# A three-stage kernel whose order comes from a planner: costs set to traced durations, first steps reordered, one integer step moved to ScalarE

## The chip, the cores and the metric

One core of one Trainium2 chip. The metric is the device time of one execution in microseconds (us). Of three runs of the kernel before, the median is 1590.36 us (1588.12 to 1594.29).

## The reference, cut to what matters

```python
def _attn_ref(q, k, v, p):            # batch 8, heads 8, seq 576, head_dim 64; p has 32 rows
    p_packed = sm_attn(p, k, v)       # 32 packed queries attend to k, v
    return sm_attn(q, p_packed, p_packed)
...
x = attn_out.transpose(0, 2, 1, 3).reshape(B * S, H * D)     # 4608 x 512
g = x @ w_gate; x = (g * sigmoid(g) * (x @ w_val)) @ w_out   # d_ff 1536
h = x @ w_in; g = where(h >= 1, h, where(h <= -1, 0, (h + 1) ** 2 / 4))
out = g @ w2_out                                             # d_ff 2048
```

All of it is float32, but the weights of the two MLPs arrive as 64-bit floats.

## The kernel before, in words

**Tiles and stages.** The attention runs in 16 "quads" (a batch and four heads). A quad has four steps: `stage_a` (scores of the packed rows and exponentials), `stage_b` (transposes and values), `stage_c` (scores of q) and `stage_d` (outputs). The two MLPs are products of 9 blocks of 512 tokens with pairs of weight columns. A "unit" (`first_unit`) is seven Strassen products of 12 matmuls, each 128x128 by 128x256 (line 1171); second products are at lines 1315 (512 columns) and 1433. Each operand is a high and a low half in float16, so every product is three matmuls. To make an operand, its block of four quarters in a `raw` buffer is scaled (`copy`, lines 392 and 396), summed into the quarters that Strassen's scheme needs (`either`, line 378), cast to the high halves (`copy`, 390 and 394) and subtracted to give the low halves (378).

**Weights.** A 64-bit weight is two 32-bit words. `from_words` makes a float32 of them: ScalarE rescales the high word (442), VectorE shifts the result left by three (445), and VectorE ors in the upper three bits of the low word (448). It runs on 128x512 at a time, 42 times for the first MLP and 32 for the second. The items of the first MLP are "in" (two columns, four such blocks), "out" and "again" (two blocks each).

**What sets the order.** The program is first recorded as operations with costs per engine, due times and dependencies; `Order.run` then plays it through with a list scheduler, picks an engine for each operation that may run on several, and emits the instructions in that order. On the chip each engine runs its list strictly in order and waits by semaphores, so a wrong cost shows up as a wait. In `copy`, `either` and `act` the costs are written as a constant and a term per column. `QUEUED` bounds how far the transfers on SP run ahead; `PORT` and `AHEAD` say when VectorE prefers an operation that does not share its port with GpSimd. `BEGIN` lists the first steps by letter and number (l load keys and values, q load queries, a to d the attention steps, w convert weights, p prepare them). `LATE` gives the place at which each further weight item of the first MLP is prepared (a place is half a unit; its items are in 1, out 1, in 2, out 2, again 0 to 2, in 3 to 5, out 3 to 5), `NEXT` and `SPACE` the places of the further quads, `CHUNKS` and `CHUNK_SPACE` those of the second MLP's weights.

Of the kernel before, what the change touches and what calls it, by code (L numbers as in the profile page):

```python
# [13 lines left out]
I32 = mybir.dt.int32  # L14
AF = mybir.ActivationFunctionType
# [27 lines left out]
class Order:  # L43
# [225 lines left out]
def packed_attention_then_two_mlps(ctx, tc, qT, kT, v, pT, w1, wo, w2, wo2, out):  # L269
# [111 lines left out]
    def copy(n, dst, src, r, w, late=None, scale=None, psum=False):  # L381
        costs = {
            "ACT": (0.05 if psum else 0.1) + (0.09 if scale else 0.0) + n * 0.00083,
            "DVE": 0.07 + (0.06 if scale else 0.0) + n * (0.00104 if psum else 0.00052),
        }

        def emit(e):
            if e == "ACT":
                if scale is None:
                    nc.scalar.copy(dst(), src())  # L390
                else:
                    nc.scalar.activation(dst(), src(), AF.Copy, scale=scale())  # L392
# [19 lines left out]
    SUM_WAIT, PREP_SUM, PREP_LO, ATT_WAIT, X_LO = 0.0, 4.8, 1.0, 4.0, 0.6  # L412
    HIDDEN_LO, BEND_WAIT = 2.0, 0.5
# [5 lines left out]
    def dma(size, dst, src, r, w, late=None):  # L419
        o.add({"SP": size / 0.3}, lambda e: nc.sync.dma_start(out=dst(), in_=src()), r, w, late)  # L420
# [8 lines left out]
    def flat(b, n=7 * N // 2, dtype=F32):  # L429
        return b.t.rearrange("p a n -> p (a n)").bitcast(dtype)[:, :n]  # L430


    def from_words(words, dst, r, w, n):

        def bits():
            return dst().bitcast(I32)  # L440

        act(n, lambda: nc.scalar.activation(
            dst(), words()[:, :, 1].bitcast(F32), AF.Prelu, scale=2.0 ** -112, alpha=-2.0 ** 32
        ), r, w, fixed=0.12)
        dve(n // 2, lambda: nc.vector.tensor_scalar(
            out=bits(), in0=bits(), scalar1=3, scalar2=None, op0=ALU.logical_shift_left,
        ), w, w, fixed=0.0, shared=True)
        dve(n, lambda: nc.vector.scalar_tensor_tensor(  # L448
            bits(), words()[:, :, 0], 29, bits(), op0=ALU.logical_shift_right, op1=ALU.bitwise_or,
        ), r + w, w, fixed=0.06, shared=True)  # L450
# [299 lines left out]
    def stage_a(i):  # L750
# [3 lines left out]
        for u in range(2):  # L754
            dve(H2, lambda u=u: nc.vector.tensor_reduce(
                t.t[:, u:u + 1], s1[u].t[:, :H2], axis=AX.X, op=ALU.max
            ), [(s1[u], 0)], [(t, u)], 1.0, 0.0)
# [118 lines left out]
    def stage_c(i):  # L876
# [11 lines left out]
        for u in range(2):  # L888
            dve(H2, lambda u=u: nc.vector.transpose(
                flat(zt, S)[:, u * H2:(u + 1) * H2], s2[u].t[:, :H2]  # L890
            ), [(s2[u], 0)], [(zt, u)], 1.0, 0.0)
        dve(S, lambda: nc.vector.tensor_reduce(t.t[:, :NTB], blocks(), axis=AX.X, op=ALU.max),
            [(zt, 0), (zt, 1)], [(t, 0)], None, 0.0)
# [3 lines left out]
            [(zt, 0)], [(zt, 0)], None, "exp", 0.1)  # L897
# [4 lines left out]
            [(zt, 0)], [(t, 1)], None, 0.0)  # L902
# [6 lines left out]
        dve(S, lambda: nc.vector.transpose(flat(z, S), flat(zt, S)), [(zt, 0)], [(z, 0)], None, 0.0)  # L909
# [59 lines left out]
    BEGIN = "l0 a0 w0 l1 p0 q0 q1 a1 b0 w1 c0 p1 b1 d0 c1 d1"  # L969

    FIRST, EARLY = 2, 2
    LATE = (0, 0.5, 4.5, 7, 18, 21, 24, 12, 26, 36, 43, 48, 52)
    LEAD, FETCH = 2, 4
    NEXT, SPACE, AHEAD = (0, 0.9, 2.1, 4.3, 6.2, 8.5, 11), 2.8, 1.2
    CHUNKS, CHUNK_SPACE, BEHIND = 61, 1.25, 0
# [784 lines left out]
```

## Time and profile before

| what | value |
|---|---|
| median of three runs | 1590.36 us |
| the profiled execution | 1590.13 us, of which the span is 1588.2 us |
| TensorE (PE) busy, share of the span | 1530.0 us, 96% |
| VectorE (DVE) busy | 1256.0 us, 79% |
| ScalarE (ACT) busy | 1000.9 us, 63% |
| GpSimd (POOL) busy | 1210.1 us, 76% |
| mean granted TensorE clock | 0.985 |

The profiled execution lies 0.23 us under the median, so a sum against it may be read as one against the median. Its 1.9 us outside the span are not seen in the profile. PE is the engine that ends the kernel; a share of 96% over the whole span hides that nearly all of its idle time lies in the first 200 us, so the table of stretches is to be read before any mean.

### The profile page before, as it was taken

How to read it: one execution, taken by the hardware profiler on the slowest of the kernel's cores; microseconds unless marked ns; L12 is line 12 of the kernel's file. 1: busy time of each engine (PE TensorE's matmuls, PEld its weight loads, DVE VectorE, ACT ScalarE, POOL GpSimd, SP SyncE). 2: the span in 40 equal slices, each digit the busy share in tenths (PEclk: the TensorE clock that was granted, in tenths of full speed). 3: DMA queues.
4: the chain of work that ended last, by engine and by line, in shares of the span. 5: the costliest groups of instructions: out<-in, count | busy, mean ns of one | idle time of the engine just before them, and what ended most of it. 6: DMA issues, size and time to landing. Idle time of an engine off the chain costs nothing.

```text
span 1588.2 us, 36548 instructions
## 1 busy us (share of the span) xinstructions
PE 1530.0 (96%) x14412; PEld 1295.4 (82%) x14412; DVE 1256.0 (79%) x2014; ACT 1000.9 (63%) x1747; POOL 1210.1 (76%) x1042
## 2 busy tenths in 40 slices
PE   5779999999999999999999999999999999999999
PEld 2446676677888889888888888888888888888888
DVE  7988888777877557788778998988777988875674
ACT  5777687767667545776676766656445555654541
POOL 4755577567986546976878998989788888986884
PEclk7889999999999999999999999999999999999999
DMA  9657886665547655977776943343533652254412
GB/s 342 201 189 262 275 289 237 235 225 189 199 136 257 239 166 191 300 263 256 265 250 219 325 149 127 106 173 121 170 100 124 226 180 97 107 188 155 139 59 80
DMA packets 145228, 310.15 MB, mean 195 GB/s; under 512 B 14752, under 2 KB 56224, under 8 KB 145056
## 3 DMA queue, kind: packets, MB, share of 16 engines
q1 hardware_dynamic: 145056, 307.81, 56.8%
q8 instruction: 113, 1.85, 0.5%
q14 instruction: 59, 0.48, 0.1%
HBM read 190.32 MB, written 117.44 MB: 194 GB/s over the span
## 4 chain that ended last, share of the span: by engine, by line
PE 84%; DVE 7%; ACT 5%; DMA 2%; issue 1%; POOL 1%; SPq 0%; ACTq 0%; DVEq 0%
PE ps L1171 46%; PE ps L1433 30%; PE ps L1315 4%; ACT op L390 1%; PE ps L741 1%; DVE op L378 1%; DMA h<-in_w 1%; DVE raw L378 1%; PE ps L940 1%; POOL op L378 1%; ACT raw L392 1%; DVE raw L448 1%; PE ps L786 0%; DVE ps L1154 0%; DVE acc L1333 0%
## 5 line engine op out<-in xcount | busy, mean ns | idle before, releaser
L1171 PE MATMUL ps<-op,op 128*128 128x256 f16 x7560 | 914.8, 273 | 6.6 <-DVE h L1154 4.1
L1171 PEld LDWEIGHTS <-op 128*128 128x128 f16 x7560 | 738.1, 98 | 108.8 <-issue 16.1
L1433 PE MATMUL ps<-op,op 128*128 128x256 f16 x4662 | 583.5, 273 | 1.0 <-POOL op L378 1.0
L378 POOL TENSOR_TENSOR op<-h,op 128x512 f16<-128x512 f32 (+2 forms) x353 | 437.7, 1257 | 125.3 <-ACT op L390 101.1
L1433 PEld LDWEIGHTS <-op 128*128 128x128 f16 x4662 | 456.0, 98 | 54.1 <-POOL op L378 1.5
L390 ACT CAST op<-h 128x512 f16<-128x512 f32 (+2 forms) x372 | 208.0, 596 | 90.4 <-POOL h L378 33.0
L378 POOL TENSOR_TENSOR raw<-raw 128x256 f32<-128x256 f32 (+1 forms) x184 | 177.3, 976 | 44.1 <-ACT raw L392 30.1
L378 POOL TENSOR_TENSOR h<-h,h 128x512 f32<-128x512 f32 (+1 forms) x178 | 203.9, 1146 | 8.2 <-DVE op L378 3.1
L1333 DVE SCALAR_TENSOR_TENSOR acc<-ps,f,acc 128x512 f32<-128x512 f32 x181 | 134.6, 744 | 71.1 <-PE ps L1433 65.9
L392 ACT ACTIVATE p<-ps,f 128x512 f32<-128x512 f32 x172 | 117.4, 686 | 104.5 <-PE ps L1171 97.3
L1546 ACT ACTIVATE ps<-m,half,f 128x512 f32<-128x512 f32 x144 | 112.3, 780 | 102.9 <-POOL m L1543 59.3
L378 POOL TENSOR_TENSOR op<-raw,op 128x512 f16<-128x512 f32 (+3 forms) x102 | 151.2, 1500 | 12.4 <-ACT op L390 10.0
L1549 DVE SCALAR_TENSOR_TENSOR h<-ps,f,h 128x512 f32<-128x512 f32 x144 | 106.3, 742 | 30.3 <-ACT ps L1546 29.8
L378 POOL TENSOR_TENSOR h<-h 128x512 f32<-128x512 f32 x69 | 90.3, 1308 | 47.5 <-DVE h L1518 30.7
L1154 DVE SCALAR_TENSOR_TENSOR h<-ps,f,p 128x512 f32<-128x512 f32 x126 | 93.5, 744 | 39.0 <-PE ps L1171 36.0
L1543 POOL TENSOR_SCALAR m<-h,f 128x512 f32<-128x512 f32 x76 | 63.2, 832 | 51.1 <-ACT ps L1546 31.6
L378 DVE TENSOR_TENSOR op<-h,op 128x512 f16<-128x512 f32 (+1 forms) x82 | 96.0, 1181 | 0.0
L390 ACT CAST op<-raw 128x512 f16<-128x512 f32 (+3 forms) x140 | 88.7, 668 | 9.6 <-POOL raw L378 5.4
L378 DVE TENSOR_TENSOR op<-raw,op 128x512 f16<-128x512 f32 (+3 forms) x66 | 89.8, 1372 | 1.4 <-ACT op L390 1.3
L1315 PE MATMUL ps<-op,op 128*128 128x512 f16 x360 | 86.9, 379 | 0.0
L392 ACT ACTIVATE u<-ps,f 128x512 f32<-128x512 f32 x90 | 61.7, 685 | 38.6 <-PE ps L1171 38.0
L378 POOL TENSOR_TENSOR op<-op,t 128x576 f32<-128x576 f32 x32 | 41.7, 1304 | 53.1 <-DVE t L906 13.4
(151 smaller groups left out, 1631.8 us busy)
## 6 DMA issues: line engine op xcount, KB each, us to landing
xsp<-op SPq DMA_DIRECT2D x72, 448.0 KB, 3.8
op<-xsp SPq DMA_DIRECT2D x72, 448.0 KB, 6.3
sums<-acc SPq DMA_DIRECT2D x88, 256.0 KB, 2.8
acc<-sums SPq DMA_DIRECT2D x88, 256.0 KB, 3.7
op<-wsp_out SPq DMA_DIRECT2D x44, 448.0 KB, 5.2
op<-wsp SPq DMA_DIRECT2D x44, 448.0 KB, 5.1
h<-in_w SPq DMA_DIRECT2D x24, 512.0 KB, 5.8
op<-in_kT SPq DMA_DIRECT2D x32, 288.0 KB, 5.3
```

The source lines that it names most:

```text
L378: lambda e: engine(e).tensor_tensor(dst(), x(), y(), op=op), r, w, late,
L390: nc.scalar.copy(dst(), src())
L392: nc.scalar.activation(dst(), src(), AF.Copy, scale=scale())
L448: dve(n, lambda: nc.vector.scalar_tensor_tensor(bits(), words()[:, :, 0], 29, bits(), op0=ALU.logical_shift_right, op1=ALU.bitwise_or,), r ...
L1154: psum_dve(T, lambda: nc.vector.scalar_tensor_tensor(dst(), lanes(bank.t), self.r(), lanes(add.t), op0=ALU.mult, op1=ALU.add), [(bank, 0), ...
L1171: nc.tensor.matmul(dst, a, b, start=start, stop=stop, skip_group_check=True)
L1315: nc.tensor.matmul(bank.t, x[:, js], y, start=first and i == 0 and m == 0, stop=last and i == 1 and m == 2,)
L1333: psum_dve(T, lambda: nc.vector.scalar_tensor_tensor(acc.t, bank.t, pw.output()(), acc.t, op0=ALU.mult, op1=ALU.add), r + [(acc, 0)], [(ac ...
L1433: nc.tensor.matmul(bank.t[:, l * N:(l + 1) * N], x, y, start=first and l == 0 and m == 0, stop=last and l == 1 and m == 2, skip_group_chec ...
L1543: o.add({"POOL": 0.85, "DVE": 0.42}, lambda e: engine(e).tensor_scalar(out=lanes(m.t), in0=dst(), scalar1=top(), scalar2=low(), op0=ALU.mi ...
L1546: act(T, lambda: nc.scalar.activation(bank.t, m.t, AF.Square, bias=half_one[:, 0:1], scale=inv()), [(m, 0), (f, 0)], [(bank, 0)], fixed=0.35)
L1549: psum_dve(T, lambda: nc.vector.scalar_tensor_tensor(dst(), lanes(bank.t), top(), dst(), op0=ALU.mult, op1=ALU.max), [(bank, 0), (h, t), ( ...
```

## The change

Four things change together. (1) The planner's costs: a copy on ACT costs 0.1 us more, the activations and several VectorE operations get another constant, a transfer runs at 0.39 instead of 0.30 (MB per us), and three of the scheduler's bounds move. (2) The order of the first steps. (3) The places of weight items, quads and chunks. (4) In `from_words` the shift of line 445 goes; a second activation turns the upper 16 bits of the low word into its top three bits, in place, and one VectorE instruction shifts and ors.

```diff
-    QUEUED = 6.4
+    QUEUED = 4.04
...
-    PORT, AHEAD = 0.1, 8.0
+    PORT, AHEAD = 0.33, 10.16
...
     def copy(n, dst, src, r, w, late=None, scale=None, psum=False):
         costs = {
-            "ACT": (0.05 if psum else 0.1) + (0.09 if scale else 0.0) + n * 0.00083,
+            "ACT": (0.16 if psum else 0.2) + (0.11 if scale else 0.0) + n * 0.00083,
...
-        o.add({"SP": size / 0.3}, lambda e: nc.sync.dma_start(out=dst(), in_=src()), r, w, late)
+        o.add({"SP": size / 0.39}, lambda e: nc.sync.dma_start(out=dst(), in_=src()), r, w, late)
...
         act(n, lambda: nc.scalar.activation(
             dst(), words()[:, :, 1].bitcast(F32), AF.Prelu, scale=2.0 ** -112, alpha=-2.0 ** 32
-        ), r, w, fixed=0.12)
-        dve(n // 2, lambda: nc.vector.tensor_scalar(
-            out=bits(), in0=bits(), scalar1=3, scalar2=None, op0=ALU.logical_shift_left,
-        ), w, w, fixed=0.0, shared=True)
+        ), r, w, fixed=0.24)
+        act(n, lambda: nc.scalar.activation(
+            words()[:, :, 0], words().bitcast(U16)[:, :, 1], AF.Copy, scale=2.0 ** -13, bias=2.0 ** -15 - 0.5
+        ), r, r, fixed=0.24)
         dve(n, lambda: nc.vector.scalar_tensor_tensor(
-            bits(), words()[:, :, 0], 29, bits(), op0=ALU.logical_shift_right, op1=ALU.bitwise_or,
+            bits(), bits(), 3, words()[:, :, 0], op0=ALU.logical_shift_left, op1=ALU.bitwise_or,
         ), r + w, w, fixed=0.06, shared=True)
...
-    BEGIN = "l0 a0 w0 l1 p0 q0 q1 a1 b0 w1 c0 p1 b1 d0 c1 d1"
+    BEGIN = "l0 l1 a0 w0 p0 q0 q1 a1 b0 w1 p1 b1 c0 d0 c1 d1"
...
-    LATE = (0, 0.5, 4.5, 7, 18, 21, 24, 12, 26, 36, 43, 48, 52)
-    LEAD, FETCH = 2, 4
-    NEXT, SPACE, AHEAD = (0, 0.9, 2.1, 4.3, 6.2, 8.5, 11), 2.8, 1.2
-    CHUNKS, CHUNK_SPACE, BEHIND = 61, 1.25, 0
+    LATE = (0, 2.5, 4.5, 7, 12, 16, 21, 24, 27, 37, 42.5, 47, 52)
+    LEAD, FETCH = 2, 5
+    NEXT, SPACE, AHEAD = (0, 0.9, 2.1, 4.3, 6, 8.3, 11), 2.8, 0.8
+    CHUNKS, CHUNK_SPACE, BEHIND = 61, 1.22, 0
```

Left out are constants of a few reductions, transposes and one exponential in `stage_a` and `stage_c` (0.07 to 0.1 us more each). Two inserted lines shift the numbers: line 448 of before is 450 now, 1171 is 1173.

Nearly every row of every list moves. Three places show what the prediction speaks of. First ACT, the start of its list (`h` holds the 64-bit words of the first weight item, `raw` the float32, `ps` PSUM tiles, `op` operands). Before:

```order
L442 ACT_TABLE_LOAD
L442 ACTIVATE raw_138<-h_142 128x512
L442 ACTIVATE raw_138<-h_143 128x512
L763 ACTIVATE op_107,t_178<-ps_155,t_178 128x288
L442 ACTIVATE raw_139<-h_144 128x512
L763 ACTIVATE op_107,t_178<-ps_156,t_178 128x288
L442 ACTIVATE raw_139<-h_145 128x512
L390 COPY op_109<-ps_157 128x512
```

Now:

```order
L444 ACT_TABLE_LOAD
L444 ACTIVATE raw_138<-h_142 128x512
L447 ACTIVATE h_142<-h_142 128x512
L444 ACTIVATE raw_138<-h_143 128x512
L447 ACTIVATE h_143<-h_143 128x512
L444 ACTIVATE raw_139<-h_144 128x512
L765 ACTIVATE op_107,t_178<-ps_155,t_178 128x288
L444 ACTIVATE raw_139<-h_145 128x512
L765 ACTIVATE op_107,t_178<-ps_156,t_178 128x288
L447 ACTIVATE h_144<-h_144 128x512
L447 ACTIVATE h_145<-h_145 128x512
```

Four activations have come in, and the first quad's exponentials (line 765, before 763) stand behind five activations of the weights instead of two. Second DVE, the same place, after its memsets. Before:

```order
L755 TENSOR_REDUCE t_178<-ps_155 128x1
L445 TENSOR_SCALAR raw_138<-raw_138 128x512
L755 TENSOR_REDUCE t_178<-ps_156 128x1
L448 SCALAR_TENSOR_TENSOR raw_138<-h_142,raw_138 128x512
L758 TENSOR_SCALAR t_178<-t_178 128x1
L445 TENSOR_SCALAR raw_138<-raw_138 128x512
L448 SCALAR_TENSOR_TENSOR raw_138<-h_143,raw_138 128x512
L445 TENSOR_SCALAR raw_139<-raw_139 128x512 x2
```

Now:

```order
L757 TENSOR_REDUCE t_178<-ps_155 128x1
L757 TENSOR_REDUCE t_178<-ps_156 128x1
L450 SCALAR_TENSOR_TENSOR raw_138<-raw_138,h_142 128x512
L760 TENSOR_SCALAR t_178<-t_178 128x1
L450 SCALAR_TENSOR_TENSOR raw_138<-raw_138,h_143 128x512
L769 TENSOR_SCALAR t_178<-t_178 128x1
L757 TENSOR_REDUCE t_179<-ps_157 128x1
L450 SCALAR_TENSOR_TENSOR raw_139<-raw_139,h_144 128x512
```

The shifts are gone, and the reductions of the second quad (`t_179`) stand earlier. Third PE, after the second products of the second unit (1315, now 1317), where the third unit starts (1171, now 1173) and a quad's `stage_b` stands (786, 805, 829; now 788, 807). Before:

```order
L1315 MATMUL ps_155<-op_126,op_104 128x512
L786 MATMUL ps_159<-ident,op_101 128x128 x4
L786 MATMUL ps_160<-ident,op_101 64x128
L805 MATMUL ps_156<-op_125,op_117 32x64 x4
L805 MATMUL ps_156<-op_137,op_117 32x64 x4
L805 MATMUL ps_156<-op_100,op_117 32x64 x12
L829 MATMUL ps_158<-ident,pp_175 128x128
L835 MATMUL ps_157<-ident,ppsq 1x128
...
L1171 MATMUL ps_161<-op_134,op_119 128x256
```

Now:

```order
L1317 MATMUL ps_156<-op_125,op_109 128x512
L788 MATMUL ps_157<-ident,op_136 128x128 x4
...
L1173 MATMUL ps_159<-op_104,op_121 128x256
...
L1173 MATMUL ps_161<-op_106,op_122 128x256
L788 MATMUL ps_155<-ident,op_136 64x128
...
L1173 MATMUL ps_161<-op_106,op_122 128x256
L807 MATMUL ps_162<-op_120,op_107 32x64 x4
```

48 products of the third unit now stand ahead of the quad's value products (807), which stood ahead of all of them.

## Rows read from the trace of the kernel before

**Rows 1.** The page: an engine's busy time; PE's and clock's rows of the 40 slices.

```profile
PE 1530.0 (96%) x14412; PEld 1295.4 (82%) x14412; DVE 1256.0 (79%) x2014; ACT 1000.9 (63%) x1747; POOL 1210.1 (76%) x1042
...
PE   5779999999999999999999999999999999999999
...
PEclk7889999999999999999999999999999999999999
```

**Rows 2.** Busy time by stretch: length, busy us (instructions) of each engine, clock, DMA.

```profile
0.00:53.70 53.70, 29.20 (x325) 15.16 (x325) 42.25 (x154) 34.77 (x80) 27.12 (x29) 0.78 0.87 295
53.70:114.40 60.70, 44.70 (x475) 29.39 (x472) 54.99 (x122) 50.19 (x99) 42.89 (x35) 0.87 0.62 210
114.40:200.00 85.60, 79.03 (x800) 54.91 (x797) 70.50 (x168) 59.95 (x115) 47.12 (x41) 0.97 0.78 262
200.00:400.00 200.00, 196.49 (x1989) 139.90 (x1988) 159.90 (x304) 153.42 (x285) 142.76 (x120) 1.00 0.69 235
400.00:1500.00 1100.00, 1096.25 (x10063) 980.74 (x10062) 877.69 (x1206) 670.09 (x1118) 893.58 (x770) 1.00 0.54 186
```

**Rows 3.** The chain that ended last, from 1570 us: start, length, what.

```profile
1569.91 14.42 PE ps L1433 x132
...
1584.36 0.75 DVE acc L1333
```

**Rows 4.** DVE in order of time, its first row after the memsets.

```profile
8.44 0.43 DVE L445 TENSOR_SCALAR raw<-raw 128x512 int32<-128x512 int32 x1 [1.83 <-ACT raw L442]
```

**Rows 5.** PE in order of time, 97 to 119 us: start, length, idle before and releaser.

```profile
106.63 1.08 PE L805 MATMUL ps<-op,op 128*32 128x64 f32 x32 [3.30 <-ACT op L390]
108.77 0.44 PE L805 MATMUL ps<-op,op 64*32 64x64 f32 x8 [1.06 <-ACT op L390]
113.93 0.48 PE L829 MATMUL ps<-ident,pp 128*128 128x128 f32 x1 [4.72 <-ACT pp L392]
...
114.41 1.06 PE L1171 MATMUL ps<-op,op 128*128 128x256 f16 x4
115.96 3.27 PE L1171 MATMUL ps<-op,op 128*128 128x256 f16 x16 [0.49 <-DVE op L378]
```

**Rows 6.** Busy time by stretch around the low clock, columns as in rows 2.

```profile
71.00:78.00 7.00, 6.15 (x41) 2.53 (x42) 5.27 (x22) 4.40 (x13) 6.34 (x7) 0.51 0.38 119
...
102.30:114.40 12.10, 2.97 (x47) 1.85 (x48) 11.49 (x14) 10.03 (x18) 11.14 (x9) 0.62 0.58 210
114.40:119.00 4.60, 4.11 (x22) 2.75 (x20) 3.25 (x5) 1.40 (x4) 2.12 (x3) 0.52 0.25 100
```

**Rows 7.** DVE's groups by form, 0 to 114.4 us: count | busy us, mean ns | idle; last line whole span.

```profile
L445 DVE TENSOR_SCALAR raw<-raw 128x512 int32<-128x512 int32 x16 | 9.4, 595 | 2.9 <-ACT raw L442 2.9
L378 DVE TENSOR_TENSOR op<-raw,op 128x512 f16<-128x512 f32 x7 | 7.8, 1111 | 0.0
L378 DVE TENSOR_TENSOR op<-raw,op 128x768 f16<-128x768 f32 x3 | 5.0, 1671 | 0.0
L378 DVE TENSOR_TENSOR op<-raw,op 128x1024 f16<-128x1024 f32 x1 | 2.4, 2367 | 0.0
...
L394 DVE CAST op<-raw 128x512 f16<-128x512 f32 x12 | 11.2, 931 | 0.0
```

**Rows 8.** ACT's groups by form, 0 to 114.4 us, columns as above; last line whole span.

```profile
L442 ACT ACTIVATE raw<-h 128x512 f32<-128x512 f32 x16 | 10.3, 668 | 6.4 <-DMA h<-in_w 6.4
L390 ACT CAST op<-raw 128x512 f16<-128x512 f32 x16 | 9.6, 624 | 2.4 <-DVE raw L378 1.4 <-POOL raw L378 1.0
L392 ACT ACTIVATE raw<-raw,a1s 128x1024 f32<-128x1024 f32 x5 | 5.7, 1146 | 0.9 <-DVE a1s L460 0.9
L390 ACT CAST op<-raw 128x768 f16<-128x768 f32 x5 | 4.1, 822 | 0.0
L390 ACT COPY op<-ps 128x512 f32<-128x512 f32 x6 | 3.5, 585 | 0.9 <-PE ps L786 0.8
...
L1546 ACT ACTIVATE ps<-m,half,f 128x512 f32<-128x512 f32 x144 | 112.3, 780 | 102.9 <-POOL m L1543 59.3
```

More of the change, by code (lines that the diff above doesn't have):

```diff
@@ L14 @@
 I32 = mybir.dt.int32
+U16 = mybir.dt.uint16
 AF = mybir.ActivationFunctionType
@@ L411, in packed_attention_then_two_mlps @@
     COPY_WAITS = {'DVE': 1.0}
-    SUM_WAIT, PREP_SUM, PREP_LO, ATT_WAIT, X_LO = 0.0, 4.8, 1.0, 4.0, 0.6
-    HIDDEN_LO, BEND_WAIT = 2.0, 0.5
+    SUM_WAIT, PREP_SUM, PREP_LO, ATT_WAIT, X_LO = 0, 4.8, 1, 4, 0.6
+    HIDDEN_LO, BEND_WAIT = 2, 0.5
     SQUARE_WAITS = {'DVE': 4.0, 'POOL': 1.0}
@@ L756, in stage_a @@
                 t.t[:, u:u + 1], s1[u].t[:, :H2], axis=AX.X, op=ALU.max
-            ), [(s1[u], 0)], [(t, u)], 1.0, 0.0)
+            ), [(s1[u], 0)], [(t, u)], 1.0, 0.07)
         dve(1, lambda: nc.vector.tensor_scalar(
@@ L890, in stage_c @@
                 flat(zt, S)[:, u * H2:(u + 1) * H2], s2[u].t[:, :H2]
-            ), [(s2[u], 0)], [(zt, u)], 1.0, 0.0)
+            ), [(s2[u], 0)], [(zt, u)], 1.0, 0.1)
         dve(S, lambda: nc.vector.tensor_reduce(t.t[:, :NTB], blocks(), axis=AX.X, op=ALU.max),
-            [(zt, 0), (zt, 1)], [(t, 0)], None, 0.0)
+            [(zt, 0), (zt, 1)], [(t, 0)], None, 0.07)
         either(S, blocks, blocks, lambda: wide(0), sub, [(zt, 0), (zt, 1), (t, 0)], [(zt, 0)], None,
@@ L896, in stage_c @@
         act(S, lambda: nc.scalar.activation(blocks(), blocks(), AF.Exp, scale=SCALE),
-            [(zt, 0)], [(zt, 0)], None, "exp", 0.1)
+            [(zt, 0)], [(zt, 0)], None, "exp", 0.2)
         s = lambda: t.t[:, NTB:2 * NTB]
         dve(S, lambda: nc.vector.tensor_reduce(s(), blocks(), axis=AX.X, op=ALU.add),
-            [(zt, 0)], [(t, 1)], None, 0.0)
+            [(zt, 0)], [(t, 1)], None, 0.07)
         dve(NTB, lambda: nc.vector.tensor_scalar(
@@ L908, in stage_c @@
                ATT_WAIT)
-        dve(S, lambda: nc.vector.transpose(flat(z, S), flat(zt, S)), [(zt, 0)], [(z, 0)], None, 0.0)
+        dve(S, lambda: nc.vector.transpose(flat(z, S), flat(zt, S)), [(zt, 0)], [(z, 0)], None, 0.1)
         z2 = zt
```

## The prediction

> **What bounds the kernel now.** The page comes first. PE is busy for 96% of the span, and the row of slices shows where the other 4% lie: slices one to three are at five and seven tenths, all later ones at nine [rows 1]. The table of stretches puts numbers on it [rows 2]. Up to 53.7 us, where the first MLP product starts, PE idles 53.7 - 29.2 = 24.5 us; from there to 114.4 us it idles 16.0 us; to 200 us 6.6 us; from 200 to 400 us 3.5 us; from 400 to 1500 us 3.8 us in 1100. So 40.5 us of some 58 us of idle time lie before 114.4 us, and whatever the change does after 200 us to engines other than PE can give back 7.3 us at most. The end is one run of products and a last sum on DVE [rows 3], which the change doesn't touch.
>
> Why PE waits early is read from the same table: up to 114.4 us DVE works 42.3 + 55.0 = 97.2 us, which is 85% of the stretch and 92% of what is left after its first work on weights at 8.4 us [rows 4]. ACT works 34.8 + 50.2 = 85.0 us, POOL 70.0 us [rows 2]. PE in order of time shows the form that the wait takes at its worst place: before the third unit PE waits 3.30, 1.06 and 4.72 us, 9.1 us together, in a quad's `stage_b` for results of ACT, and then 0.49 us for DVE [rows 5]. ACT is the name on the wait, but DVE is the engine without a pause in that stretch, 11.5 of 12.1 us, and ACT's casts waited longest for DVE's sums [rows 6, 8].
>
> **The change part by part.** I count up to the first product of the third unit, at 114.4 us, because there the early stage ends: after it PE is nearly full.
>
> *The shift on DVE.* Up to that product 16 blocks of weights are converted in both orders. Their 16 shifts took 9.4 us of DVE [rows 7]. All go: -9.4 us of DVE's work.
>
> *The new activation.* No row shows it. It has 512 columns, so the nearest rows bound it: 0.585 us for a copy out of PSUM below, 0.780 us for the square at line 1546 above [rows 8]. I take 0.668 us, the other activation that reads the same words at the same stride. ACT gains 16 x 0.668 = 10.7 us, at the bounds 9.4 or 12.5 us.
>
> At the start of ACT's list the first quad's exponentials now stand behind three more activations, so 2.0 us later at most, and PE's first transposes wait for them; I count 0, because the first MLP product, at 53.7 us, waits on DVE's later work, and take the 2.0 us into the range.
>
> *What else changes engine.* The planner now prices a 512-column cast on ACT at 0.2 + 512 x 0.00083 = 0.625 us, which the row gives as 0.624 us [rows 8]; before it believed 0.525. It therefore moves work off ACT, and the order shows what: up to the same product ACT loses four casts of 768 columns at 0.822 us, three scalings of 1024 at 1.146 us and two casts of 512 at 0.624 us, together 8.0 us. DVE gains one subtraction of 1024 columns at 2.37 us, four casts of 512 at 0.93 us and a few of under 0.8 us, and loses three subtractions of 768 columns at 1.67 us and two of 512 at 1.11 us to POOL [rows 7]: 6.1 against 7.2 us. The small ones are a dozen and partly cancel; I put them at +1.8 us by an estimate of 0.15 us each, so that +0.7 us is left, give or take 2 us. So DVE's sum falls by 8.7 us to 88.5 us, and ACT's rises by 2.7 us at most, to 87.7 us.
>
> How much of the 8.7 us reaches PE has two ends: nothing, if ACT now holds the same places, and all of it. DVE is the engine nearest to full, so I take all: **-8.7 us** by 114 us.
>
> *The order on PE.* 48 products of the third unit now stand ahead of the value products for which PE waited 9.1 us. I count nothing for that: the fifth of those products itself waited for a subtraction on DVE that ended at 115.9 us [rows 5], so in front they would have waited for it too. What it could give beyond DVE's share is the attention work that now follows, 1.08 + 0.44 + 0.48 = 2.0 us at most.
>
> *The first loads.* On SP the first 15 transfers are the same; then the two blocks of the first output weights pass one load of values, and one block of the next weights falls behind three. In the first stretch DMA is at 0.87 of its time [rows 2], so a later load shifts what waits for it, but the total is the same. I count 0, with 1 us either way.
>
> *The clock.* The granted clock was 0.51 from 71 to 78 us, 0.62 from 102.3 to 114.4 us and 0.52 from 114.4 to 119 us, so PE ran at 1.2 instead of 2.4 GHz in parts of them; the last two lie in and behind the long waits of PE [rows 5, 6]. PE's busy 6.15, 2.97 and 4.11 us there would take 3.1, 1.1 and 2.0 us less at full clock: 6.2 us. The waits removed, 8.7 of 40.5 us, are about a fifth; I take a quarter of the clock's loss back: **-1.5 us**, with 0 and -6.2 us as ends. The Trainium skill says (TensorE: Matmul & The Clock Gate, What's actually happening) that the array gets either all or half of its clock pulses by how busy it has been, so an idle stretch costs a second time in the work after it. By that rule taken at full, as if no wait were left long enough, the sum would be 4.7 us lower, 1575.3 us; the trace agrees that low clock stands behind waits, not how much of them is enough.
>
> *From 114 to 200 us.* Places move: again 0 to 2 come forward (18 to 12, 21 to 16, 24 to 21), in 3 goes back from 12 to 24. An "again" is two blocks, an "in" four, and each brings sums and casts. PE idles 6.6 us here and DVE works 70.5 of 85.6 us [rows 2]; I count 0, and 4 us either way.
>
> *After 200 us.* Here ACT gets 58 more activations and DVE loses 58 shifts. ACT worked 670 of 1100 us, PE 1096 [rows 2]: the cover is PE's own work, and if it were gone, ACT's 58 x 0.67 = 39 us would show only where ACT is on a unit's path. 0, with a gain of 4 us (half of what PE idles) or a loss of 4 us as ends.
>
> Sum, against the profiled 1590.1 us: -8.7 - 1.5 = -10.2, so **1580 us**. The median of the runs, 1590.36 us, is the same within 0.3 us.
>
> **The rivals.**
>
> *ACT takes DVE's place.* Both activations now stand before each or, on a strictly ordered engine, and PE's named waits were for ACT already [rows 5]. If half of the 10.7 us falls on the path, -8.7 becomes -3.4 and the clock gives nothing: 1586.7 us; if all does, 1592 us. For it: ACT's sum of 87.7 us is level with DVE's. Against: it was at 85.0 us before and not the full engine. The Trainium skill (ScalarE: Activation LUTs, Rules for kernel authors) advises VectorE, not ScalarE, for plain arithmetic. By the rows the step itself is dearer, 0.668 against 0.595 us [rows 7, 8], so by that rule alone the time would be 16 x 0.073 = 1.2 us longer, 1591.3 us; the trace doesn't bear it out as long as DVE is the fuller engine.
>
> *The early gain is larger.* DVE pauses for some 9 us between 8.4 and 114.4 us [rows 2, 4], and an order made with true costs may close some. With 4 us of those, 4.7 us more of clock and the 4 us of the next stretch: 1580 - 12.7 = 1567 us. For it: the planner's new prices meet the rows. Against: each needs another thing to go right.
>
> *Slower: the waits move to where PE was full.* Three "again" items now fall between 120 and 230 us, beside the splits of new blocks. One wait there like that before the third unit costs 9.1 us, and 2.0 us of clock behind it [rows 5, 6]. Two of them take 22 us: 1580 + 22 = 1602 us. It decides once PE idles about 18 us more between 114 and 230 us than before. Against: DVE has 15 us free in 85.6 [rows 2], and the converted blocks are as many.
>
> *The change doesn't do what it says.* A planner with better prices may give an order that is only different: that ends within a few us of 1590 and is counted with the first rival.
>
> **How the numbers follow.** My forecast gets 0.58, from 1573 us (the whole loss of clock and the 2.0 us of PE's order won as well) to 1586 us (half of DVE's gain and the clock's lost); the larger gain gets 0.10, ACT in DVE's place or nothing gained (1584 to 1592 us) 0.25, the moved waits 0.07. About 0.5% or 8 us is what a measurement of this kernel can tell from no change, so faster means under 1582.4 us, slower over 1598.3 us. Of the forecast 0.11 lies over 1582.4. Faster: 0.58 - 0.11 + 0.10 = 0.57. Same: 0.11 + 0.25 = 0.36. Slower: 0.07. The range goes from 1569 us (all ends of clock and next stretch, short of the last) to 1590 us (nothing gained); outside lie the slower case, a little of the first rival and the last of the larger gain, less than 0.2.
>
> **What would show each step.** Right: the first product of the third unit starts near 104 us; DVE's busy time up to it is near 88 us and ACT's near 88 us; the new activation's row says 0.6 to 0.75 us; PE idles about 31 us before it; the clock's low slices are fewer; from 200 to 1500 us PE idles 7 us as before. Wrong: the same product at 112 us with ACT busy to nine tenths (first rival), or idle time of PE over 15 us between that product and 230 us (third). If the new activation takes over 1 us, or new rows of 2 us and more appear for the casts that went to DVE, the exchange was mis-sized.

## The result, and the profile after

The changed kernel is slower. Its median is 1603.94 us (1603.16 to 1606.87, 4 runs) against 1592.03 us for the kernel before in the same session (1588.12 to 1594.29, 4 runs): ratio 1.008, 95% interval 1.0061 to 1.01. The forecast was 1580 us, the range 1569 to 1590. The profiled execution took 1603.16 us, of which the span is 1601.4 us.

The page first; its lines answer to [rows 1].

```profile
PE 1532.9 (96%) x14412; PEld 1294.6 (81%) x14412; DVE 1229.1 (77%) x1993; ACT 1015.0 (63%) x1762; POOL 1220.3 (76%) x1048
...
PE   4879989999999999999999999999999999999999
...
PEclk7899999999999999999999999999999999999999
```

Nothing in it looks 12 us slower. PE's first slice is a tenth lower, its second a tenth higher, its sixth (200 to 240 us) a tenth lower, and the clock's third slice is at nine tenths instead of eight. The stretches of [rows 2] tell more (columns as there; the early stage is cut at 107.1 us, where the third unit's first product now starts, instead of 114.4 us).

```profile
0.00:53.70 53.70, 26.77 (x309) 13.14 (x309) 37.50 (x146) 35.14 (x79) 27.46 (x29) 0.75 0.81 272
53.70:107.10 53.40, 42.31 (x447) 28.37 (x448) 51.02 (x117) 48.68 (x93) 41.58 (x35) 0.99 0.72 255
...
114.40:200.00 85.60, 81.50 (x860) 56.12 (x849) 70.47 (x171) 64.59 (x123) 53.23 (x49) 1.00 0.77 258
200.00:400.00 200.00, 191.94 (x1907) 135.50 (x1905) 150.96 (x292) 146.95 (x272) 144.83 (x118) 0.98 0.67 228
400.00:1500.00 1100.00, 1085.60 (x9940) 968.53 (x9938) 850.92 (x1182) 675.37 (x1126) 878.08 (x753) 1.00 0.53 184
500.00:900.00 400.00, 388.47 (x3567) 345.46 (x3566) 276.17 (x434) 260.15 (x451) 284.92 (x250) 1.00 0.70 240
```

Up to the third unit DVE worked 37.50 + 51.02 = 88.5 us, as forecast, ACT 83.8 us. From 200 to 400 us PE idles 8.1 us, where it idled 3.5, and from 400 to 1500 us 14.4 us, where it idled 3.8. Of the 14.4, 11.5 lie between 500 and 900 us, where it idled 1.8 before:

```profile
500.00:900.00 400.00, 398.18 (x3677) 356.33 (x3676) 303.71 (x469) 257.24 (x440) 294.94 (x257) 1.00 0.72 245
```

A stretch of the clock holds different work in two kernels, so I also count PE's products of both MLPs in order of time (a second product, twice as wide, counts as two) and compare when the one behind the first n starts; "product n" is that one. Before the change, product 240 starts at 114.4 us, 600 at 173.4, 1500 at 303.3, 2500 at 432.7, 7000 at 933.0 and 12000 at 1481.3 us. The changed kernel is ahead by 7.3 us at product 240, 9.8 at 600, 1.2 at 1500, 0.5 at 2500, and behind by 11.3 at 7000 and 13.2 at 12000. **Two losses**, then: 8.6 us between 164 and 302 us, and 11.8 us between 432 and 944 us.

At product 600 both kernels have done the same work, so the lead there is real. The line up to it, of before:

```profile
0.00:173.40 173.40, 128.06 (x1340) 81.95 (x1341) 148.36 (x392) 128.33 (x260) 105.92 (x93) 0.87 0.74 247
```

and of the changed kernel:

```profile
0.00:163.60 163.60, 123.24 (x1338) 79.84 (x1339) 136.51 (x382) 129.81 (x257) 108.74 (x98) 0.91 0.75 255
```

1340 and 1338 matmuls; PE idles 45.3 and 40.4 us, 5.0 less, and needs 4.8 us less for the work at a granted clock of 0.91 instead of 0.87. (At product 240 the comparison flatters: 43 matmuls of a quad were still to come, those that now stand behind the third unit's.)

How far that split can be trusted is seen in two of the kernels below, e8 and e10. Every engine runs the same order in them as in the changed kernel up to 475 us, so the same stretch can be read three times:

```profile
0.00:165.70 165.70, 126.73 (x1338) 81.23 (x1339) 135.28 (x382) 129.59 (x257) 107.18 (x98) 0.89 0.73 252
0.00:165.80 165.80, 126.87 (x1338) 80.92 (x1339) 136.08 (x382) 129.08 (x256) 108.75 (x98) 0.89 0.73 248
```

PE idles 39.0 and 38.9 us there, 6.4 less than before, and is busy 1.3 and 1.2 us less. So this order takes 5.0 to 6.4 us of idle time away; what comes back by the clock was 4.8 us in one execution and a quarter of that in two, and the whole lead is 7.6 to 9.8 us.

The first loss is read in the same way, from product 600 to 1500, in the changed kernel, before and in e8:

```profile
163.60:302.10 138.50, 129.74 (x1305) 92.21 (x1303) 103.09 (x217) 98.95 (x187) 89.50 (x74) 0.98 0.72 245
173.40:303.30 129.90, 125.24 (x1302) 90.65 (x1302) 106.90 (x220) 100.43 (x190) 86.30 (x74) 1.00 0.78 269
165.70:299.80 134.10, 126.57 (x1305) 90.69 (x1303) 106.66 (x217) 98.86 (x187) 89.81 (x74) 1.00 0.74 253
```

PE idles 8.8 us, before 4.7, in e8 7.5; and it is busy 4.5 us longer than before at a granted clock of 0.98, in e8 1.3 us longer at 1.00. About half of the 8.6 us comes with the order, the rest with the execution.

The new step, in the groups by form up to 107.1 us, which answer to [rows 7, 8]:

```profile
L450 DVE SCALAR_TENSOR_TENSOR raw<-raw,h 128x512 int32<-128x512 int32 x16 | 12.7, 806 | 2.6 <-ACT h L447 2.6
...
L444 ACT ACTIVATE raw<-h 128x512 f32<-128x512 f32 x16 | 10.8, 674 | 5.7 <-DMA h<-in_w 5.5
L447 ACT ACTIVATE h<-h 128x512 int32<-128x512 uint16 x16 | 10.3, 669 | 0.0
```

669 ns for the new activation against the 668 taken, and the shift-and-or costs 806 ns where the or alone cost 799. So the step did what was forecast, and the loss has to be looked for elsewhere.

It shows in ACT's groups from 500 to 900 us, where the second MLP's weights are converted. Before:

```profile
L442 ACT ACTIVATE raw<-raw 128x512 f32<-128x512 f32 x30 | 20.0, 671 | 6.5 <-DMA raw<-in_w 6.1 <-DMA raw<-in_wo 0.2
```

After:

```profile
L444 ACT ACTIVATE raw<-raw 128x512 f32<-128x512 f32 x30 | 20.3, 675 | 33.2 <-DMA raw<-in_w 18.8 <-DMA raw<-in_wo 13.6 <-DMA x2T<-acc 0.5
```

The same 30 activations, but ACT stands idle 33 us in front of them, waiting for words that have not landed. One such place, in three views of the changed kernel. SP's queue in order of time, where the load is issued:

```profile
528.19 0.37 SPq L421 DMA_DIRECT2D raw<-in_w  x1
```

ACT in order of time (last bracket: idle before, and what ended it):

```profile
531.00 0.68 ACT L393 ACTIVATE p<-ps,f 128x512 f32<-128x512 f32 x1
535.69 0.66 ACT L444 ACTIVATE raw<-raw 128x512 f32<-128x512 f32 x1 [4.01 <-DMA raw<-in_w]
536.25 0.67 ACT L393 ACTIVATE p<-ps,f 128x512 f32<-128x512 f32 x1
```

And PE:

```profile
534.72 0.82 PE L1435 MATMUL ps<-op,op 128*128 128x256 f16 x6
536.98 1.47 PE L1173 MATMUL ps<-op,op 128*128 128x256 f16 x12 [1.44 <-ACT p L393]
```

The load is issued at 528.19 and lands at 535.6, 7.4 us later. ACT's list has the conversion there, so ACT stops for 4.01 us; the eviction `p` of a PSUM tile stands behind it, whose products had ended at 532.9 us; it starts at 536.25, and PE waits 1.44 us for that tile. The wait on PE's row names ACT, the cause is a DMA two steps back.

### The profile page after: what moved, and what is told of

Its sections match the earlier page's. It is cut to its first block, busy times and chain, and to the rows that moved or that the text cites. A ratio compares the mean times of both kernels' runs of the same rounds, so it can differ in the third digit from the quotient of the medians.

```text
span 1601.4 us, 36464 instructions
## 1 busy us (share of the span) xinstructions
PE 1532.9 (96%) x14412; PEld 1294.6 (81%) x14412; DVE 1229.1 (77%) x1993; ACT 1015.0 (63%) x1762; POOL 1220.3 (76%) x1048
## 4 chain that ended last, share of the span: by engine, by line
PE 74%; DMA 7%; DVE 5%; POOL 3%; ACT 3%; issue 2%; SPq 1%; POOLq 0%; ACTq 0%; DVEq 0%
PE ps L1173 41%; PE ps L1435 27%; PE ps L1317 3%; DMA x2T<-acc 1%; DMA op<-xsp 1%; POOL raw L379 1%; DMA h<-in_wo 1%; POOL op L379 1%; PE ps L743 1%; SPq L421 1%; DMA raw<-in_w 1%; DMA raw<-w2f 1%; PE ps L942 1%; DVE op L379 1%; DMA raw<-in_wo 1%
## 5 line engine op out<-in xcount | busy, mean ns | idle before, releaser
L379 POOL TENSOR_TENSOR op<-h,op 128x512 f16<-128x512 f32 (+2 forms) x360 | 442.3, 1247 | 117.8 <-ACT op L391 101.8
L391 ACT CAST op<-h 128x512 f16<-128x512 f32 (+2 forms) x360 | 203.6, 598 | 78.6 <-POOL h L379 38.9
L379 POOL TENSOR_TENSOR raw<-raw 128x256 f32<-128x256 f32 (+1 forms) x179 | 168.0, 949 | 52.4 <-ACT raw L393 20.2
L379 POOL TENSOR_TENSOR op<-raw,op 128x512 f16<-128x512 f32 (+3 forms) x104 | 159.7, 1554 | 12.4 <-ACT op L391 8.3
L379 POOL TENSOR_TENSOR h<-h 128x512 f32<-128x512 f32 x72 | 98.9, 1373 | 46.2 <-DVE h L1520 24.4
L1156 DVE SCALAR_TENSOR_TENSOR ps<-ps,f,u 128x512 f32<-128x512 f32 x54 | 40.8, 756 | 72.4 <-PE ps L1173 55.5
L1545 POOL TENSOR_SCALAR m<-h,f 128x512 f32<-128x512 f32 x69 | 57.2, 829 | 47.9 <-ACT ps L1548 28.2
L379 DVE TENSOR_TENSOR op<-h,op 128x512 f16<-128x512 f32 (+1 forms) x75 | 91.0, 1221 | 0.0
L391 ACT CAST op<-raw 128x512 f16<-128x512 f32 (+3 forms) x124 | 80.7, 689 | 6.4 <-POOL raw L379 3.6
L1545 DVE TENSOR_SCALAR m<-h,f 128x512 f32<-128x512 f32 x75 | 64.9, 865 | 23.5 <-ACT ps L1548 23.4
```

Of the source, the lines that this page charges most:

```text
L379: lambda e: engine(e).tensor_tensor(dst(), x(), y(), op=op), r, w, late,
L1156: psum_dve(T, lambda: nc.vector.scalar_tensor_tensor(dst(), lanes(bank.t), self.r(), lanes(add.t), op0=ALU.mult, op1=ALU.add), [(bank, 0), ...
L1545: o.add({"POOL": 0.85, "DVE": 0.42}, lambda e: engine(e).tensor_scalar(out=lanes(m.t), in0=dst(), scalar1=top(), scalar2=low(), op0=ALU.mi ...
```

## The experiments

**Theories.** A: the plan now believes transfers faster than they are, and puts conversions where their words have not landed. B: the second activation per block fills ACT's list. C: the changed places. All runs in one table: ratio to the kernel before measured beside it (its median went from 1589.8 to 1592.0 us between sessions, so ratios compare better than times), lead over before at four products (minus is earlier), and the idle time of ACT, DVE and POOL together that a DMA ended from 500 to 900 us, each added up from the waits of that stretch. Leads and waits are those of one profiled execution, which lay up to 3.3 us from its kernel's median.

| run | median us | ratio, 95% interval | 600 | 2500 | 7000 | 12000 | DMA waits |
|---|---|---|---|---|---|---|---|
| before | | | 0 | 0 | 0 | 0 | 13.5 |
| changed | 1603.94 | 1.008 (1.0061, 1.01) | -9.8 | -0.5 | 11.3 | 13.2 | 46.8 |
| e1 | 1593.56 | 1.0015 (1.0003, 1.0028) | 2.4 | 3.3 | 3.0 | 4.7 | 8.1 |
| e2 | 1586.73 | 0.997 (0.9956, 0.9985) | -4.0 | -2.6 | -4.0 | -2.2 | 10.1 |
| e4 | 1608.47 | 1.0101 (1.0072, 1.013) | 3.1 | 5.8 | 15.9 | 14.9 | 44.6 |
| e5 | 1603.51 | 1.0071 (1.0045, 1.0097) | -1.5 | 2.4 | 10.2 | 10.5 | 42.9 |
| e6 | 1614.25 | 1.0144 (1.0109, 1.0178) | 3.2 | 9.2 | 21.9 | 24.1 | 42.6 |
| e7 | 1590.68 | 0.9989 (0.9974, 1.0004) | -3.9 | -1.1 | -0.4 | 0.5 | 4.5 |
| e8 | 1587.61 | 0.9977 (0.9964, 0.9989) | -7.7 | -2.8 | -3.8 | -2.6 | 6.9 |
| e9 | 1584.54 | 0.9957 (0.9942, 0.9972) | -5.1 | -3.1 | -4.6 | -5.9 | 7.0 |
| e10 | 1594.55 | 1.0012 (0.9998, 1.0025) | -7.6 | -2.1 | -0.1 | 3.3 | 23.5 |
| e11 | 1601.36 | 1.0052 (1.0032, 1.0073) | -2.2 | 3.3 | 6.0 | 10.9 | 4.6 |
| e12 | 1593.18 | 1.0003 (0.9989, 1.0017) | -7.2 | -2.5 | -1.9 | 2.9 | 26.4 |
| e13 | 1589.05 | 0.997 (0.9959, 0.9982) | -3.7 | -0.3 | -1.6 | -1.6 | 11.5 |
| e14 | 1587.87 | 0.9977 (0.9964, 0.999) | -1.9 | 3.1 | 1.6 | 0.2 | 7.7 |
| e15 | 1588.67 | 0.9981 (0.9967, 0.9994) | -1.9 | 2.0 | 0.8 | -0.2 | 8.7 |
| e16 | 1585.04 | 0.9957 (0.9943, 0.997) | -4.1 | -1.7 | -3.2 | -4.5 | 7.5 |
| e17 | 1595.83 | 1.0034 (1.002, 1.0048) | -5.6 | -1.9 | 0.2 | 5.1 | 6.0 |
| e18 | 1593.64 | 1.0015 (1.0002, 1.0028) | -0.9 | 3.4 | 1.8 | 4.1 | 9.8 |
| e19 | 1595.57 | 1.0037 (1.0025, 1.0049) | -2.9 | -0.1 | 0.9 | 5.6 | 3.5 |

### Which part: transfers, step or places (e1, e2, e4, e5)

e1, on the changed kernel (e4 is the kernel before with these two lines the other way round):

```diff
-    QUEUED = 4.04
+    QUEUED = 6.4
...
-        o.add({"SP": size / 0.39}, lambda e: nc.sync.dma_start(out=dst(), in_=src()), r, w, late)
+        o.add({"SP": size / 0.3}, lambda e: nc.sync.dma_start(out=dst(), in_=src()), r, w, late)
```

> The changed kernel with the planner's two beliefs on transfers set back (0.30 instead of 0.39 MB per us, and 6.4 instead of 4.04 us of queue); all else as changed. Theory A (the list puts conversions of weights at a place where their words have not landed, and ScalarE, strictly ordered, stands with PSUM evictions behind them): ScalarE's wait for weight words between 500 and 900 us, 33 us in the changed kernel and 6 us in the one before, falls below 12 us, PE's idle time from 200 to 1500 us falls from 22 to some 9 us, and the time to about 1590 us. Theory B (the second activation of each weight block is what fills ScalarE's list): no fall, 1600 us or more. Theory C (the places of the items and chunks): no fall either, 1600 us or more.

> The kernel before with the two beliefs on transfers alone (0.39 MB per us, 4.04 us of queue). Theory A: ScalarE waits 20 us or more for weight words between 500 and 900 us and the time rises to about 1600 us. Theories B and C: as before, 1590 us, wait for weight words near 6 us.

e2 is the kernel before with the new `from_words` alone (both activations at 0.24), e5 the changed kernel with `BEGIN`, `LATE`, `FETCH`, `NEXT`, `AHEAD` and `CHUNK_SPACE` of before.

> The kernel before with the new conversion step alone (second activation, one shift-and-or, both activations at a constant of 0.24 us); all costs, places and transfers as before. Theory A: the late waits stay small, PE idle from 200 to 1500 us near 7 to 10 us, and the early gain of VectorE shows, 1580 to 1590 us. Theory B: PE idles 20 us or more from 200 to 1500 us, 1598 us or more. Theory C: like A.

> The changed kernel with the order of the first steps and all places (weight items, quads, chunks, fetches) set back to those of before; costs, transfers and the conversion as changed. Theory C: the time returns to 1590 us or less. Theories A and B: PE still idles 18 us or more from 200 to 1500 us, 1600 us or more, and the wait for weight words stays above 20 us under A.

A is the one that stands. Taking the two beliefs out ends the loss between products 2500 and 7000 (11.8 us to -0.3), and putting them alone into the kernel before makes it (10.1 us), without the second activation and without new places. Three pairs of kernels differ in the two beliefs alone: e1 and changed by 0.65%, before and e4 by 1.01%, e13 (below) and e5 by 1.01%. e1 itself stays 3 us over the 1590 us expected; it had lost them by product 2500 (3.3). In e4 ACT waits for the scaled words as well as for the raw ones: 13.7 us and 18.7 us of its 34.8; 20 or more had been expected for the raw ones alone. B falls: the step alone is faster than before, and ACT's wait for words stays at 6.3 us. C falls for this loss: with the places back 7.8 of the 11.8 us are still lost, and the wait for words is 24.0 us (PE idles 16.5 us from 200 to 1500 us, a little under the 18 expected).

### Rate or queue, and where (e6, e7, e8)

e6 sets back only `QUEUED`, e7 only the rate. e8 sets both back behind 450 us of the plan (`now` is the time that the scheduler has played, `o.clock` the sum of PE's costs recorded so far):

```diff
-                if eng == "SP" and channel - now > self.QUEUED:
+                queued = self.QUEUED if now < 450.0 else 6.4
+                if eng == "SP" and channel - now > queued:
...
-        o.add({"SP": size / 0.39}, lambda e: nc.sync.dma_start(out=dst(), in_=src()), r, w, late)
+        o.add({"SP": size / (0.39 if o.clock < 450.0 else 0.3)}, lambda e: nc.sync.dma_start(out=dst(), in_=src()), r, w, late)
```

> The changed kernel with only the queue bound set back to 6.4 us (the rate stays at 0.39 MB per us). If the rate is what hurts (the plan believes words landed that have not), loads are still waited for over 30 us by ScalarE, VectorE and GpSimd together from 500 to 900 us (47 us in the changed kernel, 14 before, 8 with both set back) and the time stays at 1598 us or more. If the shorter queue hurts (transfers leave later than they could), under 16 us of waits and about 1592 us.

> The changed kernel with only the believed rate set back to 0.30 MB per us (the queue stays at 4.04 us). If the rate hurts: waits for loads under 16 us from 500 to 900 us and about 1592 us. If the shorter queue hurts: over 30 us of waits, 1598 us or more.

> The changed kernel with both beliefs on transfers as changed up to 450 us of the plan, and as before (0.30, 6.4) behind it. If they hurt by the second weights' conversion from 490 to 890 us alone, product 2500 is reached at 432 us as in both kernels, the 11 us lost up to product 7000 are not lost, and the time is 1589 to 1593 us. If what hurts is elsewhere (ScalarE's second activation, the chunks' places), the loss stays and the time is 1600 us or more.

For this loss it is the rate, not the queue. With the rate back the waits for loads are 4.5 us and 0.7 us are lost from 2500 to 7000; with the queue back alone the loss stays (12.7 us), and 9.2 us more are lost ahead of it. That a longer queue lets the plan put more on a channel that it believes too fast is argued, not shown. The activation's row in e7:

```profile
L444 ACT ACTIVATE raw<-raw 128x512 f32<-128x512 f32 x30 | 20.1, 670 | 4.0 <-DMA raw<-in_w 3.2 <-POOL op L379 0.4 <-DMA wsp_out<-raw 0.2
```

e8 shows the place: set back behind 450 us, the change is 0.23% faster than the kernel before, so the rate did its harm behind that point, where the waits of the table lie in the second weights' conversion. PE's line from 500 to 900 us in e8, beside 388.47 us of busy time in the changed kernel:

```profile
500.00:900.00 400.00, 398.11 (x3684) 356.98 (x3683) 278.30 (x444) 269.81 (x463) 298.48 (x262) 1.00 0.72 245
```

### By which wait (e10), and how true the rate must be (e12)

e10 leaves the rate at 0.39 and holds ACT back from unlanded words. In `from_words` of the changed kernel:

```diff
-        act(n, lambda: nc.scalar.activation(
+        o.add({"ACT": act_cost(n, 0.24)}, lambda e: nc.scalar.activation(
...
-        ), r, w, fixed=0.24)
+        ), r, w, waits={"ACT": 0.0 if o.clock < 450.0 else 3.0})
```

> The changed kernel, rate at 0.39 and all else as changed, but behind 450 us of the plan ScalarE may take the first activation on a weight's words only 3 us after the plan believes that they have landed. If ScalarE's place behind unlanded words is what the wrong rate costs: its wait for words from 500 to 900 us falls from 33 us to under 8, PE's idle time there from 11.5 us to under 5, and the time to 1589 to 1594 us. If the rate hurts through other transfers (operands, sums, scaled words) or by crowding the queue: 1599 us or more.

```profile
L444 ACT ACTIVATE raw<-raw 128x512 f32<-128x512 f32 x30 | 20.0, 668 | 3.5 <-DMA raw<-in_w 3.5
```

33.2 us of idle time before the words' activation become 3.5, PE idles 4.3 us from 500 to 900 us instead of 11.5, and the time falls from a ratio of 1.008 to 1.0012 (0.6 us over the upper end expected). Against e7, where the rate itself is back (0.9989), that is three quarters of what the rate cost. The rest fits loads that e10 doesn't hold (ACT still waits 12.1 us for `w2f`), which no run tested.

e12 gives step and costs (e9, below) a rate of 0.343, taken for the traced one. But the planner counts a load of 512 KB (524,288 bytes) as 0.5, so its 0.343 is 360 GB/s, its 0.39 is 409 and its 0.30 is 315. The stretches of [rows 2], GB/s over the share of DMA, show 336 to 344 GB/s.

> The step and the costs (1584.5 us) with a believed rate of 0.343 MB per us, which is what the traced stretches show when DMA is taken at its full share. If a rate at or under the traced one is harmless: waits for loads from 500 to 900 us under 16 us and 1582 to 1588 us. If the plan needs the slack of 0.30 because a load also waits for others: over 20 us of waits and 1590 us or more.

Both numbers of the second reading came: waits for loads rise from 7.0 to 26.4 us, and the time is over 1590. So a belief some 6% over the traced rate brings waits back, and one some 7% under it doesn't; whether the traced rate itself (0.324 in the planner's unit) is already too much, no run shows. Nor do these waits explain the time: up to product 7000 only 0.6 us are lost (-2.5 to -1.9), and the 4.8 us go later.

### The costs, and VectorE's bounds (e9, e13)

e9 is e2 with the changed costs of copies, reductions, transposes and the exponential; e13 adds `PORT, AHEAD = 0.33, 10.16`.

> The kernel before with the new conversion step and the changed costs of copies, reductions, transposes and the exponential; places, bounds and transfers as before. If true costs help by themselves: below the step alone (1586.7 us), about 1582 us. If they only make the order different: within 4 us of 1586.7 us. If they hurt by moving casts to VectorE: 1592 us or more.

> The step and the costs (1584.5 us) with the two changed bounds of VectorE's choice (0.33 and 10.16). If they are neutral: 1583 to 1587 us. If with them VectorE waits more for the shared port: 1588 us or more, GpSimd's and VectorE's shared rows longer.

e9 is with e16 the best kernel of the study, 0.43% faster than the one before. PE in its stretches:

```profile
0.00:200.00 200.00, 156.53 (x1624) 102.69 (x1625) 170.17 (x442) 148.24 (x294) 130.95 (x113) 0.90 0.76 260
200.00:432.00 232.00, 228.06 (x2274) 167.40 (x2273) 187.73 (x335) 179.34 (x318) 170.42 (x145) 1.00 0.64 222
...
500.00:900.00 400.00, 398.37 (x3689) 357.46 (x3687) 290.97 (x445) 268.07 (x465) 292.25 (x258) 1.00 0.71 245
900.00:1500.00 600.00, 599.53 (x5491) 536.86 (x5490) 496.17 (x647) 339.91 (x565) 519.44 (x443) 1.00 0.43 148
```

Its lead at product 600, 5.1 us, is still there at 12000 (5.9): from 500 to 900 us PE idles 1.6 us (1.8 before the change). The step alone (e2) is at 0.997; the costs on top of it give 0.9957, the bounds on top of those 0.997 again. Both steps are 0.13% and their intervals overlap, so neither the costs' gain nor the bounds' loss is clear of the spread. e13's 1589.05 us lie in the range put down for harm, but the shared rows are not longer, as that reading wanted: POOL's sums (line 379) take a mean of 1219 ns against 1220 in e9, DVE's 1220 against 1236. The 4.7 us that the expectation put down for true costs were not reached; 2.2 us are within what it allows for an order that is only different.

### The places (e11, e14 to e17)

All on e9. e11 takes all of them, the other four one part each:

```diff
-    BEGIN = "l0 a0 w0 l1 p0 q0 q1 a1 b0 w1 c0 p1 b1 d0 c1 d1"
+    BEGIN = "l0 l1 a0 w0 p0 q0 q1 a1 b0 w1 p1 b1 c0 d0 c1 d1"
...
-    LATE = (0, 0.5, 4.5, 7, 18, 21, 24, 12, 26, 36, 43, 48, 52)
+    LATE = (0, 2.5, 4.5, 7, 12, 16, 21, 24, 27, 37, 42.5, 47, 52)
...
-    NEXT, SPACE, AHEAD = (0, 0.9, 2.1, 4.3, 6.2, 8.5, 11), 2.8, 1.2
+    NEXT, SPACE, AHEAD = (0, 0.9, 2.1, 4.3, 6, 8.3, 11), 2.8, 0.8
...
-    LEAD, FETCH = 2, 4
+    LEAD, FETCH = 2, 5
-    CHUNKS, CHUNK_SPACE, BEHIND = 61, 1.25, 0
+    CHUNKS, CHUNK_SPACE, BEHIND = 61, 1.22, 0
```

> The step and the costs (1584.5 us) with the changed first steps, places, fetches and chunk spacing; transfers and bounds as before. If the places do harm by themselves: 1589 us or more, with PE idle from 0 to 400 us over 50 us (47 us with step and costs). If they only fit the wrong rate or are neutral: 1582 to 1587 us.

> Step and costs (1584.5 us) with the changed first steps alone. If they carry the loss: 1592 us or more, with PE idle over 51 us up to 400 us (47 us with step and costs). If neutral, as predicted: 1581 to 1588 us.

> Step and costs (1584.5 us) with the changed places of the weight items alone. If they carry the loss: 1592 us or more, with PE's idle time grown between 114 and 400 us (8 us with step and costs) to 14 us or more. If neutral: 1581 to 1588 us.

> Step and costs (1584.5 us) with the changed places of the quads and of their loads alone. If they carry the loss (loads come 0.8 instead of 1.2 places ahead, so that ScalarE and PE wait for keys): 1592 us or more, idle time of PE grown up to 400 us. If neutral: 1581 to 1588 us.

> Step and costs (1584.5 us) with the changed fetch distance and chunk spacing alone. If they carry the loss: idle time of PE from 500 to 1500 us grows from 2 to over 8 us and the time is 1590 us or more. If neutral: 1582 to 1588 us.

The ratios stand 0.95% over e9 for all places, 0.20% for the first steps, 0.24% for the items, nothing for the quads and 0.77% for fetches and chunks: 1.21% added up, so the parts roughly carry the whole. Only e11 and e17 are clear of e9 by their intervals; first steps and quads fall in the range called neutral, and the items 0.7 us above it. In e15 PE's idle time from 114 to 400 us is 11.0 us instead of 7.8, where the loss was looked for, but under the 14 expected. In e17 it is spread from 500 to 1500 us (9.6 us instead of 2.1, over the 8 expected), and it isn't the rate's wait: loads are waited for 6.0 us. PE's waits there, the longest, in e17 and then in e9:

```profile
PE ps L1435 <- POOL op L379: 3.4, 4, 1.7
PE ps L1173 <- DVE h L1156: 2.9, 2, 2.5
PE ps L621 <- ACT junk L1400: 1.3, 2, 1.0
...
PE ps L1173 <- DVE h L1156: 1.6, 1, 1.6
PE ps L1435 <- POOL op L379: 0.3, 1, 0.3
```

Whether the spacing or the fetch distance makes them, and why, is not settled. On the changed kernel the new places cost nothing that can be told (1.008 with them, e5 without them 1.0071). With the transfers set back they cost 0.45% there too: e1 has them at 1.0015, e13 is the same kernel without them at 0.997. So what the places cost depends on the other settings; by what mechanism, no run shows.

### The shorter queue and a lower rate on e9 (e18, e19)

e18 sets `QUEUED = 4.04` on e9, e19 also the rate to 0.27.

> Step and costs (1584.5 us) with the shorter queue of 4.04 us alone. If a shorter queue helps by itself, as in the two pairs: 1578 to 1583 us, with loads landing sooner after their issue. If it helped there only by repairing an order made with other places: 1584 to 1589 us.

> The same with a believed rate of 0.27 instead of 0.30 MB per us. If 0.30 still believes too much: less wait for loads from 500 to 900 us than with 0.30 (7 us) and a time under that of the run beside it. If 0.30 is slack enough, or the plan now starts loads' users too late: the same or up to 8 us more.

e18 missed both of its ranges: the shorter queue, which went with a lower time in two pairs (e6 to changed, e1 to e7), costs 0.58% here. e19 came out by its second reading: with a rate of 0.27 loads are waited for less (3.5 us) while the time stays or grows (1.0037 beside 1.0015, the intervals overlap). Each change of a bound makes another order; that the places in the tables were set for one is argued, not shown.

## Why the prediction was wrong, by its steps

- **The early stage: the sum near, partly by luck.** The forecast was -8.7 for DVE and -1.5 for the clock, -10.2 us; at product 600 the lead is 9.8 us, and 7.7 and 7.6 us in the two other traces of the same order. The idle time fell by 5.0 to 6.4 us only, so "so I take all" of DVE's 8.7 us was too much; the clock gave 4.8 us in the trace where the sum nearly fits and 1.3 and 1.2 in the others, close to the 1.5 taken. The Trainium skill (TensorE: Matmul & The Clock Gate, What's actually happening) makes the engine's clock hang on how busy it has been, so that an idle stretch costs a second time. The traces agree in kind: with less idle time went 1.2 to 4.8 us less busy time for the same work.
- **Exchange between engines: the sums held, the rows less so.** DVE worked 88.5 us as forecast, but with three more subtractions of 1024 columns (1.72 us each) where one of 2.37 us was counted, and with three casts of 768 columns (0.85 us) that were not counted: that the sum is met to the tenth is luck. ACT worked 83.8 us, under the 87.7 given as the most and under the 85.0 of before. The new activation took 669 ns.
- **First product of the third unit:** 107.1 us, not 104; PE idle before it 38.0 us, not 31.
- **Two small readings:** DVE had worked 1.84 us before 8.4 us, so its pauses up to 114.4 us were 10.6 us, not some 9; and 6.15 us of PE at a clock of 0.51 would save 3.0 us, not 3.1. Neither moves the forecast.
- **"From 114 to 200 us: 0":** held, if the stretch is taken alone (PE idles 4.1 us, before 6.6).
- **"After 200 us: 0, give or take 4": the step that failed.** From 200 to 1500 us PE idles 22.5 us instead of 7.3. I costed there only the 58 activations and shifts, whose cover was indeed there (in e2 PE idles 4.9 us). The line `size / 0.39` stood in the diff and got no term at all; it cost the 11.8 us between products 2500 and 7000, of which 0.7 are left with the rate alone set back (e7). The rows for it were in front of me: in [rows 2], GB/s over the share of DMA gives 295 / 0.87 = 339, 235 / 0.69 = 341 and 186 / 0.54 = 344 GB/s, so some 340 GB/s is what a busy channel moves in the mean of a long stretch. In the planner's unit, where 512 KB are 0.5, its 0.39 is 409 GB/s: the change took the belief from some 7% under the traced rate to some 20% over it. The Trainium skill (DMA: Bandwidth & Descriptors, Specifications) gives some 358 GB/s as a core's share of HBM. The stretches agree with that, though the traces' slices of 10 us reach 403 to 406 GB/s with reads and writes together, in e9 414: 409 is what the channel moves in its best slices, not in the mean.
- **The lead was taken as lasting, and it isn't.** The sum carried the early gain to the end without a reason given. Between products 600 and 1500 the changed kernel loses 8.6 us. In all 19 changed orders the lead at product 1500 is 4.7 us at most, however large it was at 600; the three with the largest (changed, e8, e10), which have the same order up to there, give back 8.6, 4.2 and 4.9. In the changed kernel PE's longest waits there are for DVE's sums `h` (line 1156, 1154 before), 4.0 us against 0.7. What makes them late, and why no order keeps a larger lead, stays open.
- **The slower rival** named the right sign and the wrong place: PE idles 6.7 us from 114 to 230 us, before 6.6, and it needed 18 more. Its mechanism, items at new places, cost some 0.24% where it was alone (e15, about 4 us), not clear of the spread.
- **Other rivals:** ACT didn't take DVE's place, and the larger early gain wasn't had.

## What to carry to other kernels

Every constant in a planner is a claim that the trace can test, a believed bandwidth too: divide bytes by the busy share of the queue, in the planner's own unit, before believing a rate, and stay under what comes out (here 7% under it was harmless and 6% over it was not), because one optimistic load stops an engine that runs its list in order, with everything behind it. Follow a wait past the engine that it names: PE's row said ACT, ACT's row said DMA. And what a table of places costs depends on the other settings; when several things change at once, measure them without the new tables first (here step and costs, 0.4% faster), for the new tables can take it all back (e11).

## What the runs showed of the hardware that was not expected

- A 512-KB load took about as long from issue to landing in both kernels: from 500 to 900 us a median of 5.4 us before and 5.3 now for `raw<-in_w`, 4.6 and 5.0 for `raw<-in_wo`; the one shown took 7.4 us, with eleven others issued between 526.7 and 536 us. ACT's 27 us more of waiting for words lie in when the user is put, hardly in the transfers.
- The activation on 16-bit halves read as integers, at a stride and in place, takes the time of the plain one, 669 against 674 ns. The shift-and-or of two int32 operands took 806 ns early and 1099 ns in the second weights' stretch; the or before took 799 and 958. It goes with POOL: the 17 of the 74 shift-and-ors that had POOL at work beside them for under a tenth of their time took 670 to 693 ns, and the 36 that had it for over nine tenths a mean of 1207.
- The changed kernel, e8 and e10 have the same order on every engine up to 475 us, and on PE up to product 2980 or so, and reached product 600 at 163.6, 165.7 and 165.8 us and product 2500 at 432.2, 429.9 and 430.6 us: a difference of 2 us between leads in the table tells nothing.
